# Short groups of value matmuls, value loads of three heads on GpSimd's queue, and a reciprocal in five pieces, in an attention and mixer kernel

## The chip, the cores and the metric

The kernel runs on one core of one Trainium2 chip. The metric is the time of one execution on the device in microseconds (us), lower is better. One execution of each kernel was also taken by the hardware profiler. The span on a profile's page, from the first to the last instruction, is about 1.3 us shorter than the time of the same execution. With one core there is no second die to compare with, but each execution comes with its mean granted TensorE clock. The clock is known from records of the trace. A stretch without a record counts as 1.00.

## The reference, cut to what matters

```python
mod = (silu(c) @ w_mod)                 # six rows of 640: sa, ca, ga, sb, cb, gb
h = layernorm(x) * (1 + ca) + sa
q = (h @ wq)                            # 2048 queries, 32 heads of 128
p = softmax(q @ k_cache.T * Dh ** -0.5) # 2048 keys for each head
x = x + ga * ((p @ v_cache) @ wo)
...                                     # then a mixer MLP, modulated by sb, cb, gb
```

All inputs are bf16, x is 2048 x 640, and the two caches hold 32 heads of 2048 x 128. The change concerns the attention and the modulation rows. The mixer is not touched.

## The kernel before

The program is planned in Python. Every operation is given to a scheduler with an engine, a priority key (small is early), what it reads and writes, and `need`, an operation that has to come first. TensorE follows its keys strictly. One **step** is one head with 512 queries; there are 128. Four heads make a group, and all four chunks of queries are done for a group before the next one. A step has eight **slots** (`NP = 8`). In each slot two score matmuls fill 1024 columns, ScalarE exponentiates them, and value matmuls use earlier exponentials. The query projection of the next step and the output projection of an earlier group go in between.

The keys of a head come as four transposing DMAs and its values as one plain DMA of 512 KB, all on SyncE's queue after the first head:

```python
def load_k(h, prio, gate=(), need=()):
    for i in range(4):
        dmaT(... dma_start_transpose(K_ap[b][:, i * 512:(i + 1) * 512] ..., A_k_cache[0, h, i * 512:(i + 1) * 512, :]),
             128, gate, (K[b][i],), prio + (1.6 if h == 0 and i else 0) + 0.01 * i, need)

def load_v(h, prio, eng="SP", gate=(), need=(), after=()):
    dma(eng, ... dma_start(V_ap[b][:, :, 0:128], A_v_cache[0, h] ...), 512, gate, (V[b],), prio, need, after)

load_k(0, -297.5, gate=(wm[2],))        # wm[i]: the loads of w_mod for the first modulation rows
...                                     # in load_head, for heads 2 to 4 (h = 1, 2, 3):
load_k(h, (-294, -291, -289)[h - 1], need=from_slot((0, 0, 12)[h - 1]))
load_v(h, (-292, -290, -288)[h - 1], need=from_slot((0, 0, 12)[h - 1]))
```

The activation of `c` for the later modulation rows has one reciprocal over all 640 columns on VectorE, the engine that also empties TensorE's accumulators:

```python
P.op("DVE", ... e.reciprocal(tmp[0].ap, tmp[1].ap), ..., slot + 14.0, need=from_slot(slot + 14))
```

The keys that order TensorE's work within a step:

```python
PV_SLOTS = [2, 2, 3, 2, 2, 3, 2]              # value tiles in each slot, four matmuls each
WO_SLOTS = [-1, -1, 0, 1, 2, 3, 4, 5]         # slot of each output projection matmul
key = NP * sg + 3 + WO_SLOTS[j] + 0.6 + 0.01 * j                    # output projection
q_proj(s + 1, [NP * s + 2.3 + 0.01 * kk for kk in range(KT)])       # query projection, five matmuls
key = NP * s + 3 + slot + 0.3 + 0.01 * (u - acc)                    # values
```

## Time and profile before

| | before |
|---|---|
| median of three runs | 1376.79 us (1374.85 to 1377.16) |
| 27 executions in the rounds of the experiments | 1374.6 to 1378.3 us |
| TensorE busy | 98% of the span |
| mean step with all its parts (steps 13 to 111) | 9.253 us |
| three long steps, by the ends of their query projections | 13.40, 10.63 and 8.54 us (8.76 in the prediction; see the experiments) |

TensorE is busy nearly all the time, so only two things can shorten the run: less time per matmul, or fewer stops of TensorE.

### The profile page before, as it was taken

Reading aid. Unit: us, or ns where it says so; the run is one execution under the profiler, and the core shown is the slowest. Engines: PE = TensorE matmul, PEld = TensorE weight load, DVE = VectorE, ACT = ScalarE, POOL = GpSimd, SP = SyncE. Lnnn points to the kernel's source line nnn. Section 1 sums busy time; section 2 is a strip of 40 time slices with the busy share of each in tenths; the row PEclk is TensorE's granted clock in tenths of the full one; section 3 lists DMA queues with packets and bytes.
Section 4 is the critical chain, followed back from the end, with each engine's and each line's share of the span. In section 5 each row is a group of like instructions: output and inputs, shape, how many; then the busy total and the mean of one; then the engine's idle time right before and its main releaser. Section 6 shows DMA issues by size and latency. Waiting matters only on the chain.

```text
span 1374.5 us, 29675 instructions
## 1 busy us (share of the span) xinstructions
PE 1352.1 (98%) x12865; PEld 941.7 (69%) x13099; DVE 572.6 (42%) x1436; ACT 1102.4 (80%) x1145; POOL 108.0 (8%) x94
## 2 busy tenths in 40 slices
PE   9899999999999999999999999999999999999999
PEld 7666677777767777776677777767777766655665
DVE  5454445443233323323332332333233245799563
ACT  6788888888888888888888888888888888833322
POOL 0000000000000000000000000000333237500000
PEclk9999999999999999999999999999999999999999
DMA  9562713353213322141205121422236100441120
GB/s 209 120 121 48 124 33 62 81 108 98 47 36 73 71 47 35 32 93 36 54 14 107 36 47 36 89 55 47 55 60 133 32 15 17 114 85 44 39 44 31
DMA packets 270548, 90.38 MB, mean 66 GB/s; under 512 B 250937, under 2 KB 268410, under 8 KB 270410
## 3 DMA queue, kind: packets, MB, share of 16 engines
q1 hardware_dynamic: 266874, 85.75, 30.4%
q10 hardware_dynamic: 3296, 1.67, 0.6%
q8 instruction: 104, 1.70, 0.5%
q0 software_dynamic: 240, 0.98, 0.2%
q14 instruction: 34, 0.28, 0.1%
HBM read 41.68 MB, written 2.63 MB: 32 GB/s over the span
## 4 chain that ended last, share of the span: by engine, by line
PE 95%; DMA 2%; issue 1%; DVE 1%; SPq 1%; ACT 0%
PE f_O L821 35%; PE f_S L802 29%; PE f_M L756 10%; PE f_M L726 9%; PE f_S L998 2%; PE f_M L998 2%; PE f_O L985 2%; PE f_S L985 2%; PE f_S L936 1%; PE f_S L959 1%; PE f_M L959 1%; DMA f_KV<-in_A_v_cache_dram 1%; PE f_O L936 1%; SPq L610 1%; DMA f_W<-in_w_mod_dram 0%
## 5 line engine op out<-in xcount | busy, mean ns | idle before, releaser
L804 ACT ACTIVATE f_PQ<-f_S 128x1024 bf16<-128x1024 f32 x1024 | 1041.7, 1024 | 144.3 <-PE f_S L802 113.0
L821 PEld LDWEIGHTS f_O<-f_KV,f_PQ 128*128 128x128 bf16 x8192 | 590.3, 98 | 235.5 <-DMA f_KV<-in_A_v_cache_dram 4.1
L821 PE MATMUL f_O<-f_KV,f_PQ 128*128 128x129 bf16 x8192 | 713.7, 220 | 11.2 <-DMA f_KV<-in_A_v_cache_dram 3.8
L802 PE MATMUL f_S<-f_PQ,f_KV 128*128 128x512 bf16 x1857 | 664.9, 379 | 4.1 <-DMA f_KV<-in_A_k_cache_dram 0.4
L764 DVE TENSOR_TENSOR f_y<-f_M,f_y 128x320 f32<-128x320 f32 x192 | 94.4, 492 | 504.5 <-PE f_M L756 504.5
L756 PE MATMUL f_M<-f_wo,f_OO 128*128 128x320 bf16 x992 | 272.8, 299 | 0.6 <-DVE f_y L762 0.6
L802 PEld LDWEIGHTS f_S<-f_PQ,f_KV 128*128 128x128 bf16 x2048 | 196.8, 98 | 29.8 <-ACT f_PQ L804 1.3
L726 PE MATMUL f_M<-f_hT,f_wq 128*128 128x512 bf16 (+1 forms) x609 | 169.7, 378 | 1.8 <-DVE f_tmp L767 0.2
L756 PEld LDWEIGHTS f_M<-f_wo,f_OO 128*128 128x128 bf16 x992 | 96.1, 98 | 29.4 <-DVE f_y L762 1.1
L730 DVE CAST f_PQ<-f_M 128x512 bf16<-128x512 f32 x127 | 87.8, 691 | 57.4 <-PE f_M L726 57.3
L830 DVE TENSOR_TENSOR f_OO<-f_O,f_rl 128x256 bf16<-128x256 f32 x256 | 108.3, 423 | 8.3
L538 POOL TENSOR_TENSOR f_y<-f_y,f_mod 128x640 f32<-128x640 f32 x32 | 49.1, 1543 | 785.7 <-DVE f_y L764 785.7
L726 PEld LDWEIGHTS f_M<-f_hT,f_wq 128*128 128x128 bf16 x640 | 62.4, 98 | 63.8 <-DVE f_tmp L767 0.6
L828 DVE RECIPROCAL f_rl<-f_O 128x2 f32<-128x2 f32 x256 | 43.4, 170 | 37.9 <-PE f_O L821 33.7
L988 ACT ACTIVATE f_OO<-f_S 128x512 bf16<-128x512 f32 x28 | 16.7, 597 | 43.6 <-PE f_S L985 43.6
L762 DVE COPY f_y<-f_M 128x320 f32<-128x320 f32 x32 | 15.7, 489 | 45.3 <-PE f_M L756 45.3
L499 DVE BATCH_NORM_STATS2 f_small<-f_y 128x6 f32<-128x320 f32 (+1 forms) x72 | 32.3, 478 | 1.8 <-POOL f_y L538 1.7
L998 PE MATMUL f_S<-f_KV,f_OO 128*128 128x320 bf16 x224 | 31.7, 299 | 0.0
L998 PE MATMUL f_M<-f_KV,f_OO 128*128 128x320 bf16 x224 | 31.7, 299 | 0.0
L544 ACT ACTIVATE f_xn<-f_y,f_small 128x640 bf16<-128x640 f32 x10 | 9.1, 915 | 25.7 <-DVE f_small L523 25.7
L658 DVE TENSOR_REDUCE f_small<-f_tmp 128x1 f32<-128x640 f32 x20 | 16.4, 820 | 30.3 <-ACT f_PQ L804 30.3
L988 ACT ACTIVATE f_OO<-f_O 128x512 bf16<-128x512 f32 x28 | 16.7, 596 | 14.1 <-PE f_O L985 14.1
(147 smaller groups left out, 531.6 us busy)
## 6 DMA issues: line engine op xcount, KB each, us to landing
f_KV<-in_A_v_cache_dram SPq DMA_DIRECT2D x31, 512.0 KB, 4.5
f_wo<-in_A_wo_dram SPq DMA_DIRECT2D x8, 640.0 KB, 4.2
f_wq<-in_A_wq_dram SPq DMA_DIRECT2D x7, 640.0 KB, 4.5
f_xin<-in_A_x_dram SPq DMA_DIRECT2D x13, 320.0 KB, 3.4
out_dram<-f_xin SPq DMA_DIRECT2D x15, 160.0 KB, 1.8
f_KV<-in_B_w_dram SPq DMA_DIRECT2D x5, 432.0 KB, 3.3
f_KV<-in_A_k_cache_dram SPq DMA_TRANSPOSE x128, 2.7
f_OO<-f_OO SPq DMA_TRANSPOSE x128, 2.5
```

What stands on the lines that cost most here:

```text
L538: P.op(eng, lambda e: e.tensor_tensor(out=out, in0=a, in1=b, op=op), COST[eng][0], rd, wr, prio, lat=300 if eng == "POOL" else None, dual= ...
L726: P.op("PE", lambda e, i=i, kk=kk, mm=mm, a=a, z=z: e.matmul(mm[:, 0:z - a], wq_t[g % 2][:, kk, hh * 128:(hh + 1) * 128], hT_t[ch][:, kk, ...
L730: P.op("DVE", lambda e: e.tensor_copy(q.ap, m.ap), 690, (m,), (q,), s * NP - 90)
L756: P.op("PE", lambda e, m=m, qt=qt, hf=hf, hh=hh: e.matmul(m[:, 0:HD], OT_ap[gs][:, qt, hh, :], wo_t[g % 2][:, hh, hf * HD:(hf + 1) * HD], ...
L764: P.op("DVE", lambda e, m=m, yt=yt: e.tensor_tensor(out=yt.ap, in0=m[:, 0:HD], in1=yt.ap, op=ALU.add), 490, (m, yt), (yt,), s * NP - 60)
L802: P.op("PE", lambda e, sp=sp, r=r, kt=kt: e.matmul(sp[:, r * QC:(r + 1) * QC], K_ap[b][:, kt * 128:(kt + 1) * 128], q.ap, start=True, stop ...
L804: x = P.op("ACT", lambda e, sp=sp, pt=pt: e.activation(pt.ap.rearrange("p k q -> p (k q)"), sp.ap, ACT.Exp, scale=SCALE), 1021, (sp,), (pt ...
L821: ins = e.matmul(o[bk][:, w * 129:w * 129 + 129], pt[:, r, qt * 128:(qt + 1) * 128], V_ap[b][:, u, 0:129], start=(u == 0 and w == 0), stop ...
L828: P.op("DVE", lambda e, ov=ov, i0=i0: e.reciprocal(rl_t[:, i0:i0 + 2].unsqueeze(2), ov[:, 0:258].rearrange("p (u d) -> p u d", u=2)[:, :, ...
L830: evac.append(P.op("DVE", lambda e, ov=ov, i0=i0, bk=bk: e.tensor_tensor(out=On_ap[gs][:, 2 * bk:2 * bk + 2, hh, :], in0=ov[:, 0:258].rear ...
L985: P.op("PE", lambda e, m=m, f=f, kk=kk: e.matmul(m.ap, w3_ap[:, kk, f * 128:(f + 1) * 128], nT_ap[ch][:, kk, :], start=(kk == 0), stop=(kk ...
L998: P.op("PE", lambda e, f=f, hf=hf: e.matmul(m[:, hf * 512:hf * 512 + HD], gT_ap[:, f, i * 128:(i + 1) * 128], w4_ap[f][:, hf * HD:(hf + 1) ...
```

## The change

The intent: keep at most four value matmuls in a row by putting projection matmuls between them; take the value loads of heads 2 to 4 out of the line behind the transposes; break the long reciprocal up; start the first keys earlier.

```diff
-                 128, gate, (K[b][i],), prio + ...
+                 128, gate if i or h else (wm[0],), (K[b][i],), prio + ...
-    def load_v(h, prio, eng="SP", gate=(), need=(), after=()):
+    def load_v(h, prio, gate=(), need=(), after=()):
+        eng = "POOL" if h in (1, 2, 3) else "SP"
...
-        P.op("DVE", lambda e: e.reciprocal(tmp[0].ap, tmp[1].ap), 825, ..., slot + 14.0, ...)
+        for k in range(KT):                       # five pieces of 128 columns, one per step
+            sl = slice(k * 128, (k + 1) * 128)
+            P.op("DVE", lambda e, sl=sl: e.reciprocal(tmp[0][:, sl], tmp[1][:, sl]), 900, ..., slot + 20.0 + NP * k, ...)
-            load_v(h, (-292, -290, -288)[h - 1], need=from_slot((0, 0, 12)[h - 1]))
+            load_v(h, (-290, -289, -288)[h - 1], need=from_slot((2, 9, 16)[h - 1]))
-        modulation(n, p, 80 + 40 * n)
-    mod_rows(80 + 160 + 30)
+        modulation(n, p, 120 + 40 * n)
+    mod_rows(120 + 160 + 30)
-                    key = NP * sg + 3 + WO_SLOTS[j] + 0.6 + 0.01 * j
+                    w = WO_SLOTS[j]
+                    key = NP * sg + 3 + w + (0.315 if w >= 0 and PV_SLOTS[w] == 3 else 0.6) + 0.001 * j
-            q_proj(s + 1, [NP * s + 2.3 + 0.01 * kk for kk in range(KT)])
+            q_proj(s + 1, [NP * s + (1.375 if kk == 0 and 0 < s < NS - NC * HG else 2.3) + 0.01 * kk for kk in range(KT)])
-            plan.emit(nc, es, {"SP": 24, "ACT": 8, "POOL": 1}, redo, flag, general)
+            plan.emit(nc, es, {"SP": 24, "ACT": 8, "POOL": 4}, redo, flag, general)
```

The cuts ("...") leave out unchanged arguments and the product that follows the reciprocal, which moves from slot + 20 to slot + 60.

More of the change, by code (lines that the diff above doesn't have):

```diff
@@ L610, in load_k @@
             dmaT(lambda e, i=i: e.dma_start_transpose(K_ap[b][:, i * 512:(i + 1) * 512].unsqueeze(1), A_k_cache[0, h, i * 512:(i + 1) * 512, :]),
-                 128, gate, (K[b][i],), prio + (1.6 if h == 0 and i else 0) + 0.01 * i, need)
-    def load_v(h, prio, eng="SP", gate=(), need=(), after=()):
+                 128, gate if i or h else (wm[0],), (K[b][i],), prio + (1.6 if h == 0 and i else 0) + 0.01 * i, need)
+    def load_v(h, prio, gate=(), need=(), after=()):
         b = h % NKV
+        eng = "POOL" if h in (1, 2, 3) else "SP"
         dma(eng, lambda e: e.dma_start(V_ap[b][:, :, 0:128], A_v_cache[0, h].rearrange("(t p) d -> p t d", p=128)), 512, gate, (V[b],), prio, need, after)
@@ L645, in s_rows @@
         P.op("DVE", lambda e: e.tensor_scalar_add(out=tmp[1].ap, in0=tmp[0].ap, scalar1=1.0), 600, (tmp[0],), (tmp[1],), slot + 12.0, need=from_slot(slot + 12))
-        P.op("DVE", lambda e: e.reciprocal(tmp[0].ap, tmp[1].ap), 825, (tmp[1],), (tmp[0],), slot + 14.0, need=from_slot(slot + 14))
-        P.op("DVE", lambda e: e.tensor_tensor(out=s_row.ap, in0=tmp[0].ap, in1=c_bf.ap, op=ALU.mult), 825, (tmp[0], c_bf), (s_row,), slot + 20.0, dual=True,
-             need=from_slot(slot + 20))
+        for k in range(KT):
+            sl = slice(k * 128, (k + 1) * 128)
+            P.op("DVE", lambda e, sl=sl: e.reciprocal(tmp[0][:, sl], tmp[1][:, sl]), 900, (tmp[1],), (tmp[0],), slot + 20.0 + NP * k, need=from_slot(slot + 20 + NP * k))
+        P.op("DVE", lambda e: e.tensor_tensor(out=s_row.ap, in0=tmp[0].ap, in1=c_bf.ap, op=ALU.mult), 825, (tmp[0], c_bf), (s_row,), slot + 60.0, dual=True,
+             need=from_slot(slot + 60))
     def modulation(n, p, slot):
```

## The prediction

> **What bounds the kernel now.** I read the page first for shares, then the waits of TensorE (PE) for where it stands still, then PE's own order of time around each stop, and last the stretches with the granted clock.
>
> The page says that PE is busy over the whole span and that its time goes into four kinds of matmul: values (line 821), scores (802), output projection (756), query projection (726).
>
> ```profile
> PE 1352.1 (98%) x12865; PEld 941.7 (69%) x13099; DVE 572.6 (42%) x1436; ACT 1102.4 (80%) x1145; POOL 108.0 (8%) x94
> ...
> PE 95%; DMA 2%; issue 1%; DVE 1%; SPq 1%; ACT 0%
> ```
>
> The second line is the chain that ended last: 95% of it is PE work, so all that is not PE is some 5% of 1374.5 us. Each of the 128 steps (one head, 512 queries) with all its parts takes 9.25 us from one query projection to the next, with hardly any scatter; 5 early steps without output projection take about 8.17 us. Three steps stand out. Measured by the ends of their query projections they take 13.4, 10.63 and 8.76 us. So I looked for what PE waited for in the whole run:
>
> ```profile
> PE f_O L821 <- DMA f_KV<-in_A_v_cache_dram: 3.8, 2, 3.6
> PE f_S L440 <- POOL f_ones L403: 1.0, 1, 1.0
> PE f_M L756 <- DVE f_y L762: 0.6, 1, 0.6
> PE f_S L802 <- DMA f_KV<-in_A_k_cache_dram: 0.4, 1, 0.4
> PE f_S L802 <- ACT f_PQ L804: 0.4, 2, 0.2
> PE f_O L821 <- DVE f_OO L830: 0.4, 1, 0.4
> ```
>
> The columns are: total us, times, longest. The list is short: two waits for values (3.6 and 0.2), one for the first keys, and two for VectorE. The wait of 3.6 us in order of time:
>
> ```profile
> 41.78 0.59 PE L802 MATMUL f_S<-f_PQ,f_KV 128*128 128x512 bf16 x2
> 46.00 1.05 PE L821 MATMUL f_O<-f_KV,f_PQ 128*128 128x129 bf16 x8 [3.62 <-DMA f_KV<-in_A_v_cache_dram]
> 46.84 1.06 PE L802 MATMUL f_S<-f_PQ,f_KV 128*128 128x512 bf16 x2
> 47.69 1.07 PE L821 MATMUL f_O<-f_KV,f_PQ 128*128 128x129 bf16 x8
> ```
>
> These are the values of the fourth head, needed at 42.2 us. After the wait two score matmuls take 0.85 us from start to start of what follows, where others take 0.43; the stretches 46 to 49 us show a granted clock of 0.50. The load itself is late because SyncE's queue is busy with transposes that each hold it 1.26 us:
>
> ```profile
> 39.33 1.26 SPq L610 DMA_TRANSPOSE f_KV<-in_A_k_cache_dram  x1
> 40.63 1.46 SPq L615 DMA_DIRECT2D f_KV<-in_A_v_cache_dram  x1
> ```
>
> The wait for VectorE comes from one reciprocal over 640 columns, behind which the evacuations of both kinds of sums queue:
>
> ```profile
> 105.87 4.15 DVE L646 RECIPROCAL f_tmp<-f_tmp 128x640 f32<-128x640 f32 x1 [1.78 <-ACT f_PQ L804]
> 109.94 0.43 DVE L762 COPY f_y<-f_M 128x320 f32<-128x320 f32 x1
> ```
>
> **What the Trainium skill says, and whether the trace agrees.** (1) "TensorE: Matmul & The Clock Gate", Part 1, puts PE back at half clock after an idle window of about 3.4 us and gives it back after as long a busy one; this trace agrees: idle 3.62 us, then 0.50 for some 3 us. The same page, Back-to-back issue gap, gives columns/2.4 + 2.5 ns, 56.25 ns for 129 columns; the trace has 56.7 in runs of four. (2) "DMA: Bandwidth & Descriptors", Issuing engines are not separate DMA queues: all issuing engines share the same 16 DMA engines, so another queue only saves the issuer's time. Here the issuer's time is the trouble (the transposes in front), so the move can help; but in the first 32 us the DMA engines are busy nine tenths in most slices of the page, so it does not make bytes faster. (3) "SBUF — State Buffer", section SBUF: two separate sides: GpSimd writes the descriptors of its DMAs and can't while VectorE runs a two-port operation. No run before shows such a stall: GpSimd's two loads took 0.95 and 0.86 us to issue and landed after 5.6 and 4.5 us, though VectorE was busy beside the second. (4) "VectorE: DVE Perf Modes", First, the fixed hardware budget, describes the reciprocal as an iterative divide; the trace agrees, 4.15 us against 0.82 to 0.83 us for a product or sum over 640 columns.
>
> **The change, part by part.**
>
> *Value loads of heads 2 to 4 on GpSimd's queue* (with four semaphores, so that no load waits for the one before it to land). They may go after the exponentials of slots 2, 9 and 16, by the ScalarE rows at about 17.1, 25.9 and 34.2 us; a slot is one exponential of 1.02 us. With 1 us of issue and 5.1 us to landing (median of the three early value loads), they land at about 23, 32 and 40 us; the uses are at 25.5, 33.6 and 42.2. So the fourth head's wait goes: 42.21 to 46.00 is 3.79 us. The half-clock stretch goes too: from 46.00 to 49.21 PE did two groups of 8 values and two score pairs, 3.21 us, which cost 2 x 0.455 + 2 x 0.432 = 1.77 at full clock, so 1.44 us. Sum 5.2 us, and the check: 13.4 - 8.17 = 5.23. For the second head 25.87 - 25.50 = 0.37 us of the long step 8.76 - 8.17 = 0.59; I count 0.45. SyncE's queue gets its 0.6 to 1.5 us issues back; the transposes for the second query chunk, ready at 38.47 on VectorE, come no later, though their first use moves from 40.7 to about 39.6.
>
> *First piece of keys gated on the first modulation load, not the third.* SyncE waited until 8.14 us for it, and the piece landed at 13.53. PE was idle 0.44 us before the first score; the copy of the queries on ScalarE ends at 13.35, so at most some 0.4 us comes back. I count 0.3, as the earlier transpose shares the DMA engines with the modulation loads.
>
> *Reciprocal in five pieces, one per step.* The long step gives 10.63 - 9.26 = 1.37 us (0.78 before the output projection, 0.56 before the values). A piece is 4.15/5 = 0.83 us, 0.9 with overhead, in a step in which VectorE has some 2.9 us of 9.25 to do. It is placed mid-step; I count 1.3 us back.
>
> *Value matmuls in runs of four.* In the order of the built programs a step has ten runs of four and three of eight before; after it has mostly fours, one six and one two; in the first nine steps, where score pairs stay together, most eights and twelves stay. From start to start, means of the rows between 200 and 1000 us: four values 0.2267 us; eight ahead of an output projection 0.4545; eight ahead of a score 0.4584. So breaking up an eight gains 0.001 us (twice a step) or 0.005 us (once): 0.007 us a step, over some 103 steps 0.7 us. Nothing is removed: the same number of matmuls and weight loads, and the weight loads take 69% of the span against 98%. This is the headline of the change and nearly nothing in time. What it could cost: one projection matmul (0.216 us) goes between the two last value groups, so the second output bank ends 0.22 us later. VectorE starts on it 0.46 us after PE's end now, since it is still busy with the first bank, so that is hidden.
>
> *Modulation 40 slots later*: the same work; its first use is 60 steps on. Zero.
>
> Sum: 5.2 + 0.45 + 0.3 + 1.3 + 0.7 = about 8.0 us. I take off 0.8 for what is given back in the early, tight stage: 1376.8 - 7.2 = **1369.6 us**, 0.5% faster.
>
> **The rivals.**
>
> *The values on GpSimd's queue land late.* A value load is 2048 rows of 256 bytes; GpSimd's loads so far have 512 and 640 rows of 512 bytes and more. If issue and transfer grow with the rows, say 8 us in all where I assume 6, they land at 25, 34 and 42: waits of a few tenths each, no half clock, gain 6.5 us, 1370.3. At 10 us each stalls 2 us, and the whole gain of this part is used up: 1375. For it: small rows, VectorE beside it, DMA engines at 90%. Against: the existing loads show no such slowness.
>
> *Runs of four matter more than the spacing shows.* If all 64 values of a step came at the 56.25 ns of the formula instead of about 56.8, that is 0.035 us a step, some 4 us: 1366. Against: runs of four already stand beside the eights in this trace, at 56.7.
>
> *A new wait in the steady step.* The projection takes its bank earlier and the evacuation has less slack; if it waited 0.1 us a step, 103 steps cost 10 us: 1380. Against: the rows show some 0.7 us between the end of the evacuation (601.2) and the next value matmul on that bank (601.94).
>
> **Range and chances.** All that can be won early is about 7.4 us and the steady part holds 0.7, so below 1366 needs the second rival. Late values take me to 1375. Range 1366.5 to 1374.5. A change of 2% would be 27 us; nothing here reaches it: within 2% 0.98, faster 0.01, slower 0.01.
>
> **What would show it.** Right: no wait of PE for values over 0.3 us, no stretch at 0.50 after 20 us, early steps all near 8.2, the step with the reciprocal at 9.25, ordinary steps between 9.24 and 9.25. Wrong: a wait of PE for values of heads 2 to 4 (GpSimd's issue much over 1 us); steps of 9.21 or less (runs of four do matter); steps over 9.26 or waits of PE for VectorE in every step (the third rival).

## More of the kernel before

The prediction shows the waits and the stops in order of time. Four more views of the kernel before are needed later. The first is SyncE's queue in order of time, with start and duration in us, then the line, the tiles, and the number of DMAs:

```profile
28.56 6.80 SPq L600 DMA_TRANSPOSE f_hT<-f_xn  x4
35.41 5.18 SPq L610 DMA_TRANSPOSE f_KV<-in_A_k_cache_dram  x4
```

These are the transposes for the second chunk of queries and then the four key pieces of the fourth head. The second view lists DMA issues in the stretch from 33 to 40.5 us, with the median time from issue to landing at the end of the line:

```profile
f_KV<-in_A_k_cache_dram SPq DMA_TRANSPOSE x4, 2.6
f_hT<-f_xn SPq DMA_TRANSPOSE x2, 2.7
```

The third is VectorE in order of time, at its products on that second chunk of queries:

```profile
36.77 1.70 DVE L602 TENSOR_SCALAR f_hT<-f_hT,f_small 128x512 bf16<-128x512 bf16 x5 [2.27 <-DMA f_hT<-f_xn]
```

The fourth is the first score pair of the fourth head, in TensorE's order of time. It has no wait:

```profile
38.27 0.59 PE L802 MATMUL f_S<-f_PQ,f_KV 128*128 128x512 bf16 x2
```

So before, a transpose issued in that stretch lands in under 3 us, by the median, and the fourth head's scores do not wait for it.

## The result, and the profile after

| | before | after |
|---|---|---|
| median of four executions each, same rounds | 1376.39 us | 1371.01 us |
| lowest and highest | 1374.85, 1377.16 | 1369.78, 1371.19 |
| ratio of the means, 95% interval | | 0.996, 0.9943 to 0.9978 |
| profiled execution | 1375.85 us | 1370.90 us |

A ratio here is the mean time of one kernel's runs over the mean of the other's runs of the same rounds, so it is not quite the ratio of the medians quoted beside it. The output is correct. The time fell by 5.4 us and lies in the predicted range, though it gained less than the 7.2 us predicted.

First the page's span, then the chain of work that ended last, and the top of the list of TensorE's waits (us in total, times, longest), all of the kernel after:

```profile
span 1369.6 us, 29680 instructions
```

```profile
PE 98%; issue 1%; DVE 1%; ACT 0%; POOL 0%; POOLq 0%
```

```profile
PE f_S L806 <- ACT f_PQ L808: 1.5, 3, 1.1
PE f_S L440 <- POOL f_ones L403: 1.0, 1, 1.0
PE f_M L963 <- ACT f_PQ L950: 0.3, 1, 0.3
```

In the chain the DMA share of 2% and SyncE's 1% are gone. In the list, every wait for values, for keys and for the late accumulator copies is gone. What is new is a wait of 1.1 us of a score matmul, put down to ScalarE. In TensorE's order of time it stands here:

```profile
38.50 0.62 PE L825 MATMUL f_O<-f_KV,f_PQ 128*128 128x129 bf16 x8
40.18 0.59 PE L806 MATMUL f_S<-f_PQ,f_KV 128*128 128x512 bf16 x2 [1.06 <-ACT f_PQ L808]
40.61 0.84 PE L825 MATMUL f_O<-f_KV,f_PQ 128*128 128x129 bf16 x12
```

It is the first score pair of the fourth head. To see where the 4.9 us between the two profiled executions (1375.85 and 1370.90) went, I laid the ends of the query projections of both traces side by side. The difference after minus before, added up along the run:

| up to | running difference, us | what happened since the row above |
|---|---|---|
| first score | +0.92 | TensorE's warm-up took longer (+1.14 at the first modulation matmul) |
| second query projection after it | +1.05 | |
| third | +0.68 | second head's wait for values gone, -0.37 |
| fourth | +1.91 | the new stop, +1.23 |
| fifth | -3.32 | fourth head's wait and half clock gone, -5.23 |
| step of the reciprocal | -4.70 | -1.38 |
| last query projection | -4.90 | some 100 ordinary steps, -0.20 |

The remaining 186 us, after the last query projection, are equal within 0.05 us. The first row is not the change. TensorE runs 50 dummy matmuls to warm up before the first modulation matmul. Here is that group in both traces, before and then after:

```profile
4.54 2.98 PE L440 MATMUL f_S<-f_ones 128*128 128x128 bf16 x50
```

```profile
4.54 4.13 PE L440 MATMUL f_S<-f_ones 128*128 128x128 bf16 x50
```

The same code starts at the same 4.54 us and takes 1.15 us longer: some 20 of its first matmuls start 106 to 107 ns apart where those of the kernel before start 55 to 56 ns apart. In the kernel after the last of these long gaps ends at 6.96 us, and the first record of the granted clock, 1.00, begins at 7.02; in the kernel before that record begins at 4.61. Full clock was granted 2.4 us later. Over the 13 profiles the first modulation matmul starts anywhere from 7.20 to 8.50 us, in kernels that share this code. So the one profile of the kernel after began about 1 us late by chance. A later profile of the same kernel (after_again) began at 7.28 us.

The next lines answer to those of before. SyncE's queue, one load on GpSimd's queue, VectorE's products, and the DMA issues from 33 to 41 us, all after:

```profile
28.38 6.67 SPq L600 DMA_TRANSPOSE f_hT<-f_xn  x4
35.09 5.26 SPq L610 DMA_TRANSPOSE f_KV<-in_A_k_cache_dram  x4
```

```profile
32.79 1.15 POOL L616 DMA_DIRECT2D f_KV<-in_A_v_cache_dram  x1 [6.11 <-ACT f_PQ L808]
```

```profile
39.72 1.70 DVE L602 TENSOR_SCALAR f_hT<-f_hT,f_small 128x512 bf16<-128x512 bf16 x5 [4.54 <-DMA f_hT<-f_xn]
```

```profile
f_KV<-in_A_v_cache_dram POOLq DMA_DIRECT2D x1, 512.0 KB, 6.7
...
f_KV<-in_A_k_cache_dram SPq DMA_TRANSPOSE x4, 4.1
f_hT<-f_xn SPq DMA_TRANSPOSE x2, 5.2
```

SyncE issues the same transposes, 0.2 to 0.3 us earlier than before. But they now land after 4.1 and 5.2 us (medians) instead of 2.6 and 2.7. My reading is that this is because the value load of the fourth head, issued at 32.79 on the other queue, is in flight at the same time and lands 6.7 us later. The first key piece, issued at 35.09, lands 5.0 us later, at 40.1, and the score pair that needs it starts at 40.18. Before, that piece was issued at 35.41 and the pair started at 38.27, so it took 2.9 us at most. By the program the pair depends on three things: the keys from SyncE's DMA, the queries that VectorE casts, and accumulators that ScalarE has emptied. The profile names only one. So my reading was: ScalarE is named, but the keys are the cause. The experiments test it.

The reciprocal, one of its five pieces, and an ordinary step of TensorE after the change:

```profile
109.53 0.95 DVE L649 RECIPROCAL f_tmp<-f_tmp 128x128 f32<-128x128 f32 x1 [0.20 <-ACT f_PQ L808]
```

```profile
602.69 0.38 PE L806 MATMUL f_S<-f_PQ,f_KV 128*128 128x512 bf16 x1
602.91 0.51 PE L825 MATMUL f_O<-f_KV,f_PQ 128*128 128x129 bf16 x6
603.25 0.30 PE L760 MATMUL f_M<-f_wo,f_OO 128*128 128x320 bf16 x1
603.38 0.28 PE L825 MATMUL f_O<-f_KV,f_PQ 128*128 128x129 bf16 x2
```

The order is as intended, with a six and a two left. The mean of steps 13 to 111 is 9.2515 us against 9.2533.

### The profile page after: what moved, and what is told of

Same layout as the page of the kernel before. It is cut to its first block, busy times and chain, and to the rows that moved or that the text cites. A ratio compares the mean times of both kernels' runs of the same rounds, so it can differ in the third digit from the quotient of the medians.

```text
span 1369.6 us, 29680 instructions
## 1 busy us (share of the span) xinstructions
PE 1351.2 (99%) x12865; PEld 941.9 (69%) x13099; DVE 574.0 (42%) x1440; ACT 1102.7 (81%) x1145; POOL 111.6 (8%) x97
## 4 chain that ended last, share of the span: by engine, by line
PE 98%; issue 1%; DVE 1%; ACT 0%; POOL 0%; POOLq 0%
PE f_O L825 35%; PE f_S L806 30%; PE f_M L729 10%; PE f_M L760 10%; PE f_S L1002 2%; PE f_M L1002 2%; PE f_O L989 2%; PE f_S L989 2%; PE f_S L940 1%; PE f_S L963 1%; PE f_M L963 1%; PE f_S L440 1%; PE f_O L940 1%; ACT f_PQ L808 0%; PE f_S L760 0%
## 5 line engine op out<-in xcount | busy, mean ns | idle before, releaser
L825 PEld LDWEIGHTS f_O<-f_KV,f_PQ 128*128 128x128 bf16 x8192 | 617.2, 98 | 248.1 <-DVE f_OO L834 0.2
L825 PE MATMUL f_O<-f_KV,f_PQ 128*128 128x129 bf16 x8192 | 762.0, 220 | 7.0
L806 PE MATMUL f_S<-f_PQ,f_KV 128*128 128x512 bf16 x1858 | 647.5, 379 | 4.8 <-ACT f_PQ L808 1.5
L806 PEld LDWEIGHTS f_S<-f_PQ,f_KV 128*128 128x128 bf16 x2048 | 187.1, 97 | 13.8 <-ACT f_PQ L808 2.5
```

Source lines behind the costliest of these rows:

```text
L806: P.op("PE", lambda e, sp=sp, r=r, kt=kt: e.matmul(sp[:, r * QC:(r + 1) * QC], K_ap[b][:, kt * 128:(kt + 1) * 128], q.ap, start=True, stop ...
L825: ins = e.matmul(o[bk][:, w * 129:w * 129 + 129], pt[:, r, qt * 128:(qt + 1) * 128], V_ap[b][:, u, 0:129], start=(u == 0 and w == 0), stop ...
```

## The experiments

Theory: nearly all of the gain is three stops early in the run, above all the fourth head's values; part of it is given back because the moved value load slows the transposes that SyncE issues in the same moment. Rivals: the new stop belongs to ScalarE or to the new TensorE order; or the order of matmuls itself brings the gain. The experiments were in three groups, and a group shares its runs of the kernel before. Eleven kernels ran, on three chips, all with correct output:

| label | median, us | executions | before, same rounds | ratio | 95% interval |
|---|---|---|---|---|---|
| order_only | 1376.35 | 5 | 1376.49 | 0.9996 | 0.9982 to 1.001 |
| values_only | 1372.84 | 4 | 1376.49 | 0.9974 | 0.9959 to 0.9989 |
| recip_only | 1375.37 | 4 | 1376.49 | 0.9992 | 0.9977 to 1.0008 |
| no_order | 1370.68 | 5 | 1376.49 | 0.9955 | 0.9942 to 0.9969 |
| no_values | 1374.56 | 4 | 1376.33 | 0.9989 | 0.9974 to 1.0004 |
| v_slot18 | 1370.12 | 5 | 1376.33 | 0.9954 | 0.994 to 0.9968 |
| v_slot19 | 1369.73 | 5 | 1376.33 | 0.9954 | 0.9941 to 0.9968 |
| k_first_piece | 1369.13 | 5 | 1376.33 | 0.9954 | 0.994 to 0.9967 |
| after_again | 1370.63 | 5 | 1376.46 | 0.9955 | 0.9942 to 0.9969 |
| k_first_v19 | 1368.85 | 5 | 1376.46 | 0.9943 | 0.993 to 0.9957 |
| k_first_no_gate | 1369.82 | 5 | 1376.46 | 0.9953 | 0.9939 to 0.9966 |

The interval is about 4 us wide, so steps of the traces have to settle what is smaller. In these lists of early steps, "step 1" runs from the first to the second query projection after the first score; a step without any stop takes 8.17 us. In nine of the traces one record is missing, that of the last matmul of the query projection which ends step 1: the next matmul starts 430 to 432 ns after the last one recorded, where it is 215 to 216 ns elsewhere. So the end of step 1 is taken 0.216 us later there. Without this the kernel before shows 7.96 and 8.76 us in place of 8.17 and 8.54, which is how the prediction came to 8.76.

| label | steps 1 to 5, us | stop at the fourth head's first scores | wait for its values |
|---|---|---|---|
| before | 8.17, 8.54, 8.17, 13.40, 8.17 | none | 3.62 |
| order_only | 8.78, 8.81, 8.17, 11.44, 8.17 | none | 3.10 |
| recip_only | 8.17, 8.85, 8.17, 11.60, 8.17 | none | 3.25 |
| no_values | 9.43, 8.28, 8.33, 11.59, 8.17 | none | 3.24 |
| values_only | 8.31, 8.17, 9.95, 8.17, 8.17 | 1.61 | none |
| after | 8.32, 8.17, 9.40, 8.17, 8.17 | 1.06 | none |
| after_again | 8.23, 8.17, 9.86, 8.17, 8.17 | 1.52 | none |
| no_order | 8.97, 8.17, 9.83, 8.17, 8.17 | 1.49 | none |
| v_slot18 | 8.17, 8.17, 10.00, 8.17, 8.17 | 1.66 | none |
| v_slot19 | 8.42, 8.17, 8.31, 8.18, 8.17 | none | none |
| k_first_piece | 8.17, 8.17, 8.17, 8.18, 8.17 | none | none |
| k_first_v19 | 8.52, 8.17, 8.17, 8.17, 8.17 | none | none |
| k_first_no_gate | 8.17, 8.17, 8.89, 8.38, 8.17 | none, but one of 0.77 later | none |

The stops in the steps 1 over 8.17 us are not explained here. They change from one profile of the same kernel to the next (8.32 and 8.23 us for the kernel after). The largest are 0.61 us for query weights in no_values and 0.64 us at a score pair in no_order.

### order_only

The kernel before with the new TensorE order and nothing else:

```diff
-                    key = NP * sg + 3 + WO_SLOTS[j] + 0.6 + 0.01 * j
+                    w = WO_SLOTS[j]
+                    key = NP * sg + 3 + w + (0.315 if w >= 0 and PV_SLOTS[w] == 3 else 0.6) + 0.001 * j
-            q_proj(s + 1, [NP * s + 2.3 + 0.01 * kk for kk in range(KT)])
+            q_proj(s + 1, [NP * s + (1.375 if kk == 0 and 0 < s < NS - NC * HG else 2.3) + 0.01 * kk for kk in range(KT)])
```

> The kernel before with the new order of matmuls alone (first projection matmul between the last value groups, output projection inside the groups of twelve). My theory: a run of eight costs at most 0.005 us more than two fours, and the trace of the changed kernel has lost only 0.2 us over 100 steps, so an ordinary step stays at 9.25 us and the time at about 1376.2, within 0.5 us of the kernel before. Rival (long runs of values cost PE time): a step of 9.22 us or less and 1372 to 1373. The early wait for values and the step of 10.6 us stay in both.

The time did not move: 1376.35 against 1376.49 us. The ordinary step became 9.2514 us, 0.0019 less than before, which is 0.2 us over some 100 steps. The headline of the change is worth nothing that the clock can show.

This profile brought something else. The fourth head's wait for values is there, as before:

```profile
46.45 0.63 PE L822 MATMUL f_O<-f_KV,f_PQ 128*128 128x129 bf16 x8 [3.10 <-DMA f_KV<-in_A_v_cache_dram]
```

But the half clock after it is not. Here is the microsecond from 47 to 48 in the view by stretches, of the kernel before and then of order_only (stretch and length, busy TensorE, weight loads, VectorE, ScalarE, GpSimd with counts, granted clock, DMA share, GB/s):

```profile
47.00:48.00 1.00, 1.00 (x6) 0.46 (x4) 0.00 (x0) 0.07 (x1) 0.00 (x0) 0.50 1.02 356
```

```profile
47.00:48.00 1.00, 1.00 (x13) 0.66 (x11) 0.00 (x0) 0.46 (x1) 0.00 (x0) 1.00 1.05 378
```

This step took 11.44 us where the profile before had 13.40. So was the 1.4 us of half clock, which my prediction counted, only an accident of one profile? The profiles alone suggest it: three of the four kernels that keep the wait show a step of 11.4 to 11.6 us. But every execution has its mean clock on record, and half clock for the 3.41 us that the record of the kernel before has (45.57 to 48.99 us) lowers the mean by 0.5 x 3.41 / 1375 = 0.0012, which shows as 0.999 instead of 1.000:

| | executions | below 1.000 | mean time of those below, us | mean time at 1.000, us |
|---|---|---|---|---|
| before | 27 | 24 | 1376.8 | 1375.1 |
| order_only | 5 | 3 | 1376.5 | 1374.6 |
| recip_only | 4 | 3 | 1375.5 | 1373.4 |
| no_values | 4 | 2 | 1375.6 | 1373.6 |
| the eight other kernels, with values on GpSimd (after and after_again are one) | 43 | 1 | 1371.5 | 1370.4 |

Where the wait exists, 32 of 40 executions have the lower clock and are about 2 us longer; where it doesn't, 1 of 43. So the half clock is the usual case, and the three profiles without it fell on the rarer executions. (The 27 of the kernel before are those in the rounds of the experiments.) Why some executions escape was not isolated. The waits without half clock were 3.10 to 3.25 us long, the one with it 3.62. The clock records give a hint. Each one that ends with a change of clock lasts 3.41 us or a whole multiple of it (40.96, 1365.33 and 1368.74 us are 12, 400 and 401 times 3.4133), so the changes of one execution lie on a grid of 3.41 us. In the kernel before, one stretch of this grid, 42.16 to 45.57 us, holds no start of a matmul, and the half clock follows it. In the three other profiles the stop lies across two stretches, and each holds at least 6 starts. So where the stop falls on the grid may decide. That is not shown: a stop of 3.1 to 3.8 us that fell anywhere on the grid would cover a whole stretch far less often than in 32 of 40 executions.

### values_only

The kernel before with the value loads alone moved:

```diff
+        eng = "POOL" if h in (1, 2, 3) else "SP"
-            load_v(h, (-292, -290, -288)[h - 1], need=from_slot((0, 0, 12)[h - 1]))
+            load_v(h, (-290, -289, -288)[h - 1], need=from_slot((2, 9, 16)[h - 1]))
-            plan.emit(nc, es, {"SP": 24, "ACT": 8, "POOL": 1}, redo, flag, general)
+            plan.emit(nc, es, {"SP": 24, "ACT": 8, "POOL": 4}, redo, flag, general)
```

> The kernel before with the three value loads on GpSimd's queue alone. My theory: the step of 13.4 us becomes 8.17 (5.2 us won), the second head's wait goes (0.2 to 0.4), and a new wait of about 1.1 us comes at the first scores of the fourth head, because its first keys now land after 5 us in place of 2.6, sharing the DMA engines with the fourth values: 1376.4 - 4.3 = 1372.1. Rival (the loss in the changed kernel is from the moved order of matmuls or the gate, not from the loads): no such wait, 1370.9.

The gain is 3.65 us by the medians, and this is the one part whose interval lies clear of 1. The wait for values is gone, and the new stop of 1.61 us at the fourth head's first scores is there, though TensorE's order is the old one. So the stop comes with the value loads, not with the order. By the steps: 13.40 - 8.17 = 5.23 us saved, 8.54 - 8.17 = 0.37 saved, 9.95 - 8.17 = 1.78 given back, net 3.8 us, close to what was timed. This edit changes the queue, the moment of release and the semaphores of the loads together; which of them is needed was not separated.

### recip_only

The kernel before with the reciprocal in five pieces and the modulation 40 slots later, as in the diff of the change.

> The kernel before with the reciprocal in five pieces (and the modulation 40 slots later, which belongs to it) alone. My theory: the step of 10.63 us becomes 9.26, nothing else moves: 1376.4 - 1.4 = 1375.0. Rival (the stall only moves to five smaller ones): five steps of 9.3 to 9.5 us, and a gain under 0.7 us.

The step of 10.63 us became 9.26, so the 1.37 us came back in full. The medians differ by 1.1 us, within the interval's width. A piece takes 0.95 us and hides beside TensorE's work.

### no_order

The kernel after with TensorE's old keys (the reverse of order_only).

> The changed kernel with the old order of matmuls. My theory: as the changed kernel within 0.5 us, 1371.2, ordinary steps 9.25 us; the wait for the fourth head's keys stays. Rival (runs of four are worth 3 to 4 us): 1374 to 1375. Second rival (the new order, by asking for the fourth head's queries and scores at another time, makes the wait for keys): the wait goes and 1370.0.

1370.68 us, against 1371.01 and 1370.63 for the kernel after in its two series. The ordinary step is 9.2533 us again. Both ways round, the order moves the step by 0.0018 to 0.0019 us. In the trace after, four value matmuls take 0.2297 us to the start of a following query projection and 0.2271 to the start of a score; a six takes 0.3431 and a two 0.1126. In the trace before a four took 0.2267. I read this as a small cost of leaving a value group that is paid at each end of a group: cutting groups moves it rather than removes it.

### no_values

The kernel after with the value loads back on SyncE's queue (the reverse of values_only).

> The changed kernel with the value loads back on SyncE's queue. My theory: the wait for the fourth head's values is back (3 to 4 us, with or without a stretch at half clock), the wait for its keys gone, the reciprocal's gain and the 0.2 us of the order kept: 1376.4 - 1.4 - 0.2 = 1374.8. Rival (the parts work together, say because the earlier keys gate needs the loads moved): below 1373.5.

The wait for values returns (3.24 us), the time is 1374.56 us, and the stop at the fourth head's first scores is gone. It keeps the reciprocal, the order and the early keys, and is 1.8 us faster than before by the medians.

### v_slot18 and v_slot19

The kernel after with the fourth head's value load released two or three exponentials later:

```diff
-            load_v(h, (-290, -289, -288)[h - 1], need=from_slot((2, 9, 16)[h - 1]))
+            load_v(h, (-290, -289, -288)[h - 1], need=from_slot((2, 9, 18)[h - 1]))
```

(`19` for the other).

> The changed kernel with the fourth head's values two slots later (after the exponential of slot 18 in place of 16, some 2 us). My theory: the stop of 1.1 to 1.6 us before the first scores of the fourth head, which the profile puts down to ScalarE, is the landing of that head's keys, slowed to 5 us by the value load ahead of them. Two us later the keys' first piece lands within 3 us again and the stop falls to under 0.3 us; the values then land near 42 us, just before their use at about 43: a step of 8.2 to 8.5 us in place of 9.4, time about 1370.0. Rival (ScalarE, as the profile has it, or the moved order): the stop stays over 1 us, 1371.0.

> The same with three slots later (slot 19). My theory: keys as in the run with slot 18, but the values now land 0.5 to 1 us after their use at about 43, so that PE waits for values again by that much, and the time is 1370.3 to 1371. Rival (keys are not the cause): the stop before the scores stays over 1 us and a wait for values is added: 1372.

The two expectations missed in opposite directions, and this made the pair useful. Each trace, v_slot18 first, at the value load of GpSimd and the keys of SyncE, and for v_slot18 the score pair too:

```profile
33.78 1.15 POOL L616 DMA_DIRECT2D f_KV<-in_A_v_cache_dram  x1 [8.12 <-ACT f_PQ L808]
```

```profile
33.89 5.20 SPq L610 DMA_TRANSPOSE f_KV<-in_A_k_cache_dram  x4
```

```profile
39.61 0.59 PE L806 MATMUL f_S<-f_PQ,f_KV 128*128 128x512 bf16 x2 [1.66 <-issue]
```

```profile
36.15 1.15 POOL L616 DMA_DIRECT2D f_KV<-in_A_v_cache_dram  x1 [9.67 <-ACT f_PQ L808]
```

```profile
34.66 5.18 SPq L610 DMA_TRANSPOSE f_KV<-in_A_k_cache_dram  x4
```

In v_slot18 the two are issued within 0.11 us of each other; the first key piece lands 5.6 us later and the stop stays, this time put down to "issue". In v_slot19 the keys have 1.5 us to themselves; the piece lands after 3.8 us and there is no stop. The values come in time all the same. What matters is whether the piece is mostly through when the value load starts: the second piece of v_slot19, issued at 35.97, only 0.18 us ahead of the load, again took 5.1 us. The name that the profile gives the wait (ScalarE here, "issue" there) says nothing of it. The landing does: in all five traces with the stop (values_only, after, after_again, no_order, v_slot18) the score pair starts 0.09 to 0.10 us after the first piece has landed, at 39.99, 40.09, 39.24, 40.52 and 39.52 us. VectorE, the third possible cause, falls too: in v_slot18 its products had ended at 37.00. In the times of the runs the two kernels can't be told apart (means 1370.21 and 1370.12 us), and that v_slot18 met its expected 1370.0 while its stop stayed was luck.

### k_first_piece

The kernel after with only the first key piece of the fourth head issued earlier, among the third head's key pieces, with the value loads as in the change:

```diff
-                 128, gate if i or h else (wm[0],), (K[b][i],), prio + (1.6 if h == 0 and i else 0) + 0.01 * i, need)
+                 128, gate if i or h else (wm[0],), (K[b][i],), -400 + 0.01 * i if h == 3 and i < 1 else prio + (1.6 if h == 0 and i else 0) + 0.01 * i,
+                 from_slot(6) if h == 3 and i < 1 else need)
```

> The changed kernel with the first piece of the fourth head's keys put ahead of the transposes of the second query chunk on SyncE's queue. My theory: the keys land some 6 us before their use and the stop before the scores goes; the transposes of the query chunk start 1 us later and VectorE's five products after them (39.7 to 41.4 us now) end near 42.5, where the projection that reads them would start at about 41: a new wait of 0.5 to 1.5 us takes its place, time 1370.3 to 1371.3. Rival (ScalarE): the stop stays.

The waits of TensorE in this profile, top of the list:

```profile
PE f_S L440 <- POOL f_ones L403: 1.0, 1, 1.0
PE f_S L806 <- ACT f_PQ L808: 0.4, 2, 0.2
```

The stop is gone, all five early steps are 8.17 to 8.18 us, and ScalarE, order and values were left as they were. With the pair above, this shows that the stop was the late landing of that piece. The wait for the second query chunk that I had feared did not come: VectorE's products ran at 38.28 to 39.99 us, in time. The five times (1368.34 to 1371.46) scatter more than the median of 1369.13 suggests; the mean is 1369.79. One of the five, 1371.46 us, is the execution with the clock below 1.000 in the table above, and its cause is not known.

### after_again, k_first_v19 and k_first_no_gate

Three kernels in the same rounds on one chip: the kernel after unchanged; k_first_piece together with slot 19; and k_first_piece with the first head's keys gated on the third modulation load again, as before the change (`gate` in place of `gate if i or h else (wm[0],)`).

> The changed kernel itself once more, on the chip and in the rounds of the three that follow. If the stop before the fourth head's scores belongs to the kernel and is no chance of one profile, it is here again: a step of 9.3 to 10 us, time 1370.5 to 1371.5. Rival (it was chance): all early steps at 8.2 to 8.4 and 1369.5.

> Both remedies together: the first piece of the fourth head's keys early and its values after slot 19. My theory: they remove the same stop, so together they give no more than either: all early steps 8.17 to 8.4 us and 1369.5, some 1.3 us under the changed kernel of the same rounds. Rival (two different losses): 1368.5 or less.

> The kernel with the keys' first piece early, with the first head's keys gated on the third modulation load again, as before the change. My theory: the wait of 0.4 us for the first keys is back and the stretch from the last modulation matmul to the first score goes from some 4.5 us to 4.9; in the time 0.3 us, which the scatter of the start hides. Rival (the earlier transpose slows the modulation loads): the modulation matmuls end earlier than 8.9 us and the time is the same or less.

k_first_v19 is the best version: 1368.85 us median, with its slowest execution (1369.84) below the fastest of after_again (1370.09). By the means it is 1370.54 - 1369.11 = 1.4 us faster than the change, and 7.7 us faster than the kernel before. Its score pair in the trace, where the kernel after stops:

```profile
38.76 0.59 PE L806 MATMUL f_S<-f_PQ,f_KV 128*128 128x512 bf16 x2
```

For the gate, I compared the time from the start of the last group of 30 modulation matmuls to the first score. The record of the first score is missing in eight traces, where the rest come 0.216 us later; this is taken off. In seven profiles with the early gate it is then 4.43 or 4.44 us (4.73 in an eighth, v_slot19, whose group itself took 0.3 us longer), in four with the old gate 4.59 to 4.85, among them k_first_no_gate with 4.73. (recip_only is left out, since in it the modulation matmuls themselves waited for a load.) So the early gate removes about 0.3 us, but the 1.3 us of scatter in the warm-up hides it in the total: the medians of k_first_no_gate and k_first_piece, 1369.82 and 1369.13 us, are from different rounds and prove nothing. k_first_no_gate has another stop:

```profile
40.89 0.39 PE L825 MATMUL f_O<-f_KV,f_PQ 128*128 128x129 bf16 x4 [0.77 <-DMA f_KV<-in_A_k_cache_dram]
```

In k_first_piece a projection matmul on the second query chunk stands just ahead of this value group; here its record is missing from the trace, and the profile puts the wait down to keys. VectorE's products on that chunk began at 40.20 us in this trace, after 5.78 us of waiting for its transposes, against 38.28 in k_first_piece. So I take it for the wait for the second query chunk, which I had feared for k_first_piece. The trace supports it: the projection's weight load is recorded at 40.66 us and the first product ended at 40.61. No run tests it, and why the transposes came later here than in k_first_piece is not known. In k_first_v19 the products began at 36.74 us: with the value load behind the transposes, both are early.

## Why the prediction was right or wrong

**Right: what bounds the kernel, and where the gain is.** The stops of TensorE early on carried it, and the order of matmuls carried nothing. The term for the fourth head's values was 5.2 us. It measured 5.23 in the pair of profiles, half clock included, and the clocks of single executions show that this is the usual case and not the luck of one profile. In the rarer executions the term is 3.3 to 3.4, by the steps of 11.44 and 11.60 us.

**Right: second head and reciprocal.** 0.37 us where I counted 0.45, and 1.37 to 1.38 where I counted 1.3. The 0.59 us from which I rounded down to 0.45 was misread: 0.22 of it is the missing record, and the 0.37 of the wait was all there was. A piece costs 0.95 us where I said 0.83, 0.9 with overhead, which did not matter.

**Right: the rivals that fell.** Values on GpSimd's queue did take longer than I assumed, 6.5, 8.0 and 6.7 us to landing where I had 6 in all, so the rival of late values was right about the duration. The issue took 1.15 to 1.19 us, and no use of these values waited. The rival of runs of four, at 4 us, fell with order_only and no_order. No ordinary step grew a wait.

**Wrong: "the transposes for the second query chunk, ready at 38.47 on VectorE, come no later".** They came later: the products ended at 38.47 and now end at 41.42 us, because the transposes shared the DMA engines with the value load. In the kernel after that alone stopped nothing. But the same step of reasoning covered the fourth head's keys, which I did not look at, and there it cost 1.06 to 1.7 us. I had taken off 0.8 us for "what is given back" without naming a place. The prediction itself said that all queues share the DMA engines; it used this only to doubt whether the values would come sooner, and not to ask whose data would come later. The sign "early steps all near 8.2" failed for this: one took 9.40.

**Wrong in size: the order of matmuls.** 0.7 us predicted from the spacing of eights, 0.2 measured. The term assumed that cutting an eight removes its excess; by the spacings after, the excess goes with the ends of the groups.

**Right in kind, not visible in the time: the gate.** About 0.3 us in the traces, as counted, but hidden in the scatter of the warm-up. Of the wait of 0.44 us from which I counted, 0.22 is the missing record of the first score.

The sum with the measured terms: 5.2 + 0.4 + 1.4 + 0.2 less 1.2 to 1.7 given back is 5.5 to 6.0 us. The two series of the kernel after gave 5.4 (1376.39 to 1371.01) and 5.8 us (1376.46 to 1370.63) by the medians. So the 7.2 us predicted was too much by the order (0.5), the larger give-back (0.4 to 0.9), and the gate (0.3) that the time does not show. What stays open: what decides whether an execution gets the half clock after the wait, and what sets the moment at which full clock is granted at the start.

## What to carry to other kernels

When a load moves to another queue, list every transfer that will be in flight beside it and which of those is needed first; a large load issued just ahead of a small urgent one delays it. Here this held across two queues, and on one: in the kernel before, the transpose issued at 28.56 us, behind a value load of 27.93 on the same queue, landed after 5.13 us, the next three after 2.65 to 2.79. Issuing the urgent piece first can win back what the move gave away. If a wait is attributed to an engine that had long been done, look up what else the instruction waits for, and use the mean clock of every single execution before calling something in one profile typical or an accident. Before reading a step from the end of a matmul group, count the group's records: one that is missing here made 0.22 us.

## What the Trainium skill lacked or had wrong

- "DMA: Bandwidth & Descriptors", Issuing engines are not separate DMA queues, says that the DMAs of all issuing engines run on the same DMA engines, and that issuing on several only saves the sequencer's time, "which is usually small relative to the DMA itself". The first half fits: a key piece went from 2.9 us at most to 5.0 us when a value load was in flight on another queue. The second half did not fit here: each transpose held SyncE for some 1.3 us, and this queueing made one value load late enough to stop TensorE for 3.6 us.
- "TensorE: Matmul & The Clock Gate", Part 1, gives about 500 ns either way for how far the moment of full speed varies between runs. Here TensorE starts at 1.00 us in all 13 profiles, and the last gap of over 100 ns between warm-up matmuls ends anywhere from 3.96 to 6.96 us.
- No page that I consulted has that the clock record of a trace can begin only with the first grant of full clock (4.61 us in the kernel before, 7.02 in the kernel after), so that a mean clock counts the half-speed start as 1.00.
- No page that I consulted has how often a stop of TensorE of some 3.4 us brings half clock: here 32 of 40 executions of kernels whose profiles have a stop of 3.10 to 3.62 us, at a cost of about 2 us each.
- No page that I consulted has that a wait on several semaphores may be put down to the wrong one. Here a wait for a DMA was put down to ScalarE in one kernel (1.06 us) and to "issue" in another (1.66 us).
